# Attention with two feed-forward layers on one core: feed-forward products in whole blocks of four chunks, and attention's memory used again

## The chip, the core and the metric

One Trainium2 chip, one of its eight cores. The metric is the device time of one execution in microseconds; the median of several runs is compared. A profile is one execution more, taken by the hardware profiler. Engines: TensorE (PE, its weight loads PEld), VectorE (DVE), ScalarE (ACT), GpSimd (POOL), and the sync queue (SP), which issues the DMAs.

## What is computed

Block-sparse attention (2 x 8 heads, 768 positions, head size 64; a local window of 16 plus 24 block summaries of keys and values), then two feed-forward layers of 1,536 tokens, 512 wide, 2,048 hidden:

```python
x = attention(q, k, v)              # (B*S, H*D) = (1536, 512)
h = x @ w_in;  g = h * clip(h + 3, 0, 6) / 6;  x = g @ w_out     # first layer
h = x @ w_in2; g = h * cos(h);                 out = g @ w_out2  # second layer
```

Inputs are float64 for the weights. Each operand of a feed-forward product is split in a rounded high part and a low part, and three matmuls (high x high, high x low, low x high) stand for one product.

## The kernel before

**Tiling.** Tokens are cut in 3 blocks j of 512, the 2,048 hidden columns in 16 chunks of 128, and the chunks in 4 groups g of 4. The feed-forward work is a list of items (layer L, group g, block j, chunk c), lines 696 to 706: for each layer, for each group, for each block, the 4 chunks. The first block's items are cut in half, and so is the very last item (`cut`). With 2 layers x 4 groups x 3 blocks there are 24 blocks of 4 chunks.

**One item.** `g1` (line 728) is the first product: 4 steps of 3 matmuls (lines 738 to 740) into one PSUM bank `h` or `a`. `post` (line 747) turns the bank into the two parts of g: in the second layer ScalarE scales (L770), a rounding step on GpSimd or VectorE (L782), two VectorE steps (L774), two on ScalarE (L770), a VectorE product with the bank (L788), a rounded copy on ScalarE or GpSimd (L357, L359: high part) and a subtraction on VectorE or GpSimd (L364: low part). `g2` (line 796) is the second product: for each of 4 banks `acc`, 3 matmuls (line 815). A bank adds up over the 4 chunks of a block; after the fourth chunk `evac` (line 824) copies it (L357) or adds it (L837) to a part in SBUF, and at a layer's last group splits it for the next layer or sends it out.

**Weights.** `weights` (line 656) loads each chunk's two halves (`w_in`, `w_out`) as float64 words and builds high and low float32 parts: ScalarE (L676) and VectorE (L680, L685) into `cf`, a copy (L357 or L359) and a subtraction (L364) into `w`. Half 0 serves the first product, half 1 the second. All three blocks of a group use the same 4 weight tiles.

**Buffers.** PSUM has 8 banks: 4 `acc`, 2 `h`, 2 `a`. In SBUF there are 6 weight tiles `w` (`GS + 2`), 3 tiles `g`, one `n` and one `r` (odd items use `kr` and `va` of attention in their place), 2 `raw`, one `cu`, one `cf`. All are in one pool `cp` for the whole kernel.

**What sets the order.** Nothing is scheduled on the chip. Every operation is given to a planner (`Plan`) with the engines it may run on, a duration for each, a priority (smaller is earlier), what it reads and writes, and the buffers that it takes. `order` (line 221) runs a list scheduler over these durations; `refine` repeats it with due times as priorities for all but TensorE's operations and keeps the best plan; `run` (line 303) writes the instructions in that order, and each engine carries out its own in that order, waiting where it must. Priorities of the feed-forward work come from `vt` (line 710): item n of the list has a time, `IT` = 5.2 apart; its first product has that time, its second product that plus `pp` and `lag1` or `lag2` (line 859). So first and second products of single chunks take turns, with the second some items behind:

```python
for n, it in enumerate(items):
    pr = vt(it)
    h = g1(it, pr, late)
    gb = post(it, h, pr + T["pp"], late)
    g2(it, gb, pr + T["pp"] + T["lag2" if L else "lag1"])
```

Attention is 24 units of two query tiles, with priorities `A0 + AS * ...` (lines 624 to 650); feed-forward items of the first blocks fill in between. Token block 2 needs the last units.

Of the kernel before, what the change touches and what calls it, by code (L numbers as in the profile page):

```python
# [18 lines left out]
P = 128  # L19
# [28 lines left out]
def consts():  # L48
# [17 lines left out]
    late=16, cut=1, d0=0.9, warm=9, tail=1, qa=1, na=10, vy=3, split=1, lagq=0, nz=3, nq=3, nraw=2, ncf=1, n=5,  # L66
# [21 lines left out]
class Slots:  # L88
    def __init__(self, tiles, fifo=True, bank=False):
        self.tiles, self.fifo, self.bank = tiles, fifo, bank  # L90
        self.free = list(range(len(tiles)))
        self.made = self.given = 0


class Op:
    __slots__ = ("engs", "fn", "prio", "seq", "wait", "after", "ready", "takes", "uses", "start", "eng", "took")


class Plan:


    AFTER = {"PE": 0.2, "ACT": 0.145, "DVE": 0.13, "POOL": 0.1, "DMA": 0.95}
    TO_PE = {"PE": 0.0, "ACT": 0.28, "DVE": 0.25, "POOL": 0.15, "DMA": 0.95}
    LOAD = {"PE": 1.0, "ACT": 1.0, "DVE": T["DVE"], "POOL": T["POOL"], "DMA": 1.0}

    def __init__(self):
        self.ops, self.writer, self.readers = [], {}, {}

    def op(self, engs, fn, prio, r=(), w=(), take=()):
        o = Op()  # L110
        o.engs, o.fn, o.prio, o.seq = engs, fn, prio, len(self.ops)
# [36 lines left out]
    def reset(self):  # L148
        for o in self.ops:
            o.wait, o.ready, o.start, o.eng = 0, 0.0, None, None  # L150
            for x in o.uses:
                x.uses = 0
                x.slot = None
                x.cls.free = list(range(len(x.cls.tiles)))
                x.cls.given = 0
# [65 lines left out]
    def order(self):  # L221
# [13 lines left out]
        push(T["d0"], "free", None)  # L235
        for o in self.ops:
            if not o.wait:
                push(0.0, "ready", o)
        order = []
        while events:  # L240
            now = events[0][0]
            while events and events[0][0] <= now + 1e-9:
# [4 lines left out]
                elif what == "release":  # L247
                    x.cls.free.append(x.slot)
            for e in names:
# [28 lines left out]
                cost = o.engs[e] * (2.0 if e == "PE" and now < T["cold"] else 1.0)  # L278
                o.start, o.eng = now, e
# [9 lines left out]
                push(free[e], "free", None)  # L289
                for a in o.after:  # L290
# [12 lines left out]
    def run(self):  # L303
        self.refine()
        for o in self.order():
            o.fn(o.eng)


@with_exitstack
def body(ctx: ExitStack, tc: tile.TileContext, q, k, v, w_in1, w_out1, w_in2, w_out2, ident_d, mask_d, avg_d, out):  # L310
# [4 lines left out]
    pp = ctx.enter_context(tc.tile_pool(name="pp", bufs=1, space=bass.MemoryType.PSUM))  # L315

    def slots(name, n, shape, dtype=F32, fifo=True, pool=cp):
        return Slots([pool.tile(shape, dtype, name=f"{name}{i}") for i in range(n)], fifo, pool is not cp)

    ident = cp.tile([P, P], F32, name="ident")  # L320
    mask = cp.tile([P, 3, NK + CK], F32, name="mask")
    avg = cp.tile([P, AW], F32, name="avg")
# [7 lines left out]
    c_qz = slots("qz", T["nz"], [P, 2, HT * P])  # L330
    c_vc = slots("vc", 4, [P, TB, P])
    c_kr = slots("kr", 2, [P, TB, P])
    c_qr = slots("qr", T["nq"], [P, HT, P])
# [3 lines left out]
    c_vt = slots("vt", 1, [96, 4, D])  # L337
    c_e = slots("e", 4, [P, 2, NE])
    c_sm = slots("sm", 6, [P, 4])
    c_pt = slots("pt", 3, [P, 3, P])  # L340
# [41 lines left out]
    op = pl.op  # L382

# [5 lines left out]
    def load_consts():  # L389
# [9 lines left out]
        op({"POOL": 1.13}, variants, T["mask"], r=["mask"], w=["masks"])  # L399
# [31 lines left out]
    def fill_vc(b, p, vc, prio):  # L431
        for o in range(2):
            f = slice(D * o, D * o + D)
            rr = slice(32 + 32 * o, 64 + 32 * o)
            op({"POOL": 0.48},
# [6 lines left out]
    def vsum_pe(b, p, va, prio):  # L442
# [8 lines left out]
        op({"PE": 0.215 * TB}, mm, prio, r=["avg", (va, 0), (va, 1)], w=[bank], take=[bank])  # L451
        for o in range(2):
            f = slice(D * o, D * o + D)
            op({"ACT": 0.11, "DVE": 0.13}, lambda e, f=f: copy(e, vs[b][f, p, :], bank.t[f, f]), prio,
               r=[bank], w=[("vs", b, p, o)])

    def vsum(b, hh, prio):
        src = v[b, 4 * hh:4 * hh + 4].rearrange("h (n t) d -> (h n) (t d)", t=BLK)
        vt = Buf(c_vt)
        for u, (t0, n) in enumerate(((0, 12), (12, 12), (24, 8))):  # L460
# [7 lines left out]
            op({"DVE": 0.07 + 0.067 * n},  # L468
# [19 lines left out]
    def k_prep(b, p, kr, prio, banks):  # L488
# [33 lines left out]
        op({"POOL": 1.5}, edges, prio + 0.2, r=[(kw, "own", t0) for t0, _ in KCUT], w=[(kw, "edge")])  # L522
# [5 lines left out]
        op({"POOL": 0.56}, sums, prio + 0.2, r=[(ks, t0) for t0, _ in KCUT], w=[(kw, "sum")])  # L528
# [16 lines left out]
    def att(b, t, p, kw, z, va, vc, prio, banks):  # L545
# [18 lines left out]
        for o in range(2):  # L564
# [17 lines left out]
            {"POOL": 0.16},  # L582
# [8 lines left out]
            {"POOL": 0.755, "DVE": 0.455},  # L591
# [4 lines left out]
            prio, r=[(sm, 2), (sm, 3)], w=[(e_, 0), (e_, 1)],  # L596
# [8 lines left out]
        op({"ACT": 0.37, "DVE": 0.46},  # L605
# [13 lines left out]
        op({"ACT": 0.16, "DVE": 0.2}, lambda e: copy(e, hi, tp.t[:, 3 * P:4 * P]), prio, r=[(tp, 1)],  # L619
           w=[("xh", j, p, i)])  # L620
        op({"DVE": 0.2}, lambda e: sub(e, lo, tp.t[:, 3 * P:4 * P], hi), prio, r=[(tp, 1), ("xh", j, p, i)],
# [29 lines left out]


# [3 lines left out]
    def weights(c, prio):  # L656
# [3 lines left out]
        for half in range(2):  # L660
# [7 lines left out]
            else:  # L668
# [6 lines left out]
            op({"ACT": 0.52},  # L675
# [7 lines left out]
               prio, r=[raw], w=[f], take=[f])  # L683
            op({"DVE": 0.6},
# [4 lines left out]
            op({"POOL": 0.6, "ACT": 0.52}, lambda e, f=f, a=a: copy(e, w.t[:, 0, a], f.t), prio, r=[f],  # L689
               w=[(w, half, 0)], take=[w])  # L690
            op({"POOL": 1.23, "DVE": 0.6}, lambda e, f=f, a=a: sub(e, w.t[:, 1, a], f.t, w.t[:, 0, a]), prio,
               r=[f, (w, half, 0)], w=[(w, half, 1)])
# [35 lines left out]
    def g1(it, pr, late):  # L728
# [4 lines left out]
        for kk in range(KT):  # L733
# [8 lines left out]
            op({"PE": 0.65 * (y - x) / TOK}, mm, pr,  # L742
# [4 lines left out]
    def post(it, hb, pr, late):  # L747
# [21 lines left out]
        def act(func, out, in_, pr, fixed, rd, wr, take=(), **kw):  # L769
            op({"ACT": t(fixed, 0.425)}, lambda e: nc.scalar.activation(out=out(), in_=in_(), func=func, **kw), pr,  # L770
               r=rd, w=wr, take=take)

        def stt(s, out, a, b, o0, o1, rd, take=()):
            op({"DVE": t(0.07, 0.53)}, lambda e: nc.vector.scalar_tensor_tensor(  # L774
# [5 lines left out]
        else:  # L780
            act(ACTF.Identity, n, h, pr, 0.146, [hb], [nb], [nb], scale=1.0 / (2.0 * math.pi), bias=bias[:, 1:2])
            op({"POOL": t(0.16, 0.43), "DVE": t(0.07, 0.265)}, lambda e: eng[e].tensor_scalar(  # L782
                out=n(), in0=n(), scalar1=1.0, scalar2=-MAGIC, op0=ALU.mult, op1=ALU.add), pr, w=[nb])
            stt(-C1, r, n, h, ALU.mult, ALU.add, [nb, hb], [rb])
            stt(-C2, r, n, r, ALU.mult, ALU.add, [nb])
            act(ACTF.Abs, r, r, pr, 0.094, [], [rb])
            act(ACTF.Sin, r, r, pr, 0.185, [], [rb], scale=-1.0, bias=bias[:, 2:3])
            op({"DVE": t(0.07, 0.53)}, lambda e: nc.vector.tensor_tensor(out=r(), in0=r(), in1=h(), op=ALU.mult),  # L788
               pr, r=[hb], w=[rb])
        op({"ACT": t(0.095, 0.425), "POOL": t(0.16, 0.43)}, lambda e: copy(e, hi(), r()), pr, r=[rb], w=[(gb, 0)],  # L790
           take=[gb])
        op({"DVE": t(0.07, 0.53), "POOL": t(0.15, 1.08)}, lambda e: sub(e, lo(), r(), hi()), pr,
           r=[rb, (gb, 0)], w=[(gb, 1)])
        return gb

    def g2(it, gb, pr):
        L, g, j, c, x, y = it
        w = wb[L * NCH + g * GS + c]
        for m in range(4) if L == 0 else range(x // P, y // P):
# [18 lines left out]
            op({"PE": 0.65 * (1 if L else (y - x) / TOK)}, mm, pr,  # L818
# [5 lines left out]
    def evac(L, g, j, m, acc, pr):  # L824
        key, pt, take = part_of(j, m)
        if g == 0:
            op({"ACT": 0.48, "DVE": 0.6}, lambda e: copy(e, pt(), acc.t), pr, r=[acc], w=[key], take=take)
# [13 lines left out]
        if L == 0:  # L841
            hi, lo = xh[j][:, m, :], xl[j][:, m, :]
            op({"ACT": 0.52, "POOL": 0.6}, lambda e: copy(e, hi, pt()), pr, r=[key],
               w=[("xh", j, m, i) for i in range(QT)])
            op({"DVE": 0.6, "POOL": 1.23}, lambda e: sub(e, lo, pt(), hi), pr,
               r=[key, *(("xh", j, m, i) for i in range(QT))], w=[("xl", j, m, i) for i in range(QT)])
# [3 lines left out]

    for n, it in enumerate(items):
        L, g, j, c, x, _ = it
        pr = vt(it)
        if j == 0 and x == 0:
# [4 lines left out]
        g2(it, gb, pr + T["pp"] + T["lag2" if L else "lag1"])  # L859

    pl.run()

# [21 lines left out]
```

## Time and profile before

| | |
|---|---|
| time, median of 3 runs | 667.12 us (666.59 to 668.02) |
| profiled execution: its own time | 668.72 us |
| profiled execution: span, first to last instruction | 666.9 us |
| mean granted TensorE clock | 0.992 |
| TensorE matmuls busy | 641.6 us, 96% of the span |
| VectorE busy | 406.1 us, 61% |
| ScalarE busy | 346.1 us, 52% |
| GpSimd busy | 308.8 us, 46% |

Matmul records are longer than the time from one to the next, since matmuls are pipelined; starts are to be compared, not lengths. A busy share is a mean over stages that have different limits, so it is read by stage. "<-" behind a row names what an engine waited for last.

### The profile page before, as it was taken

To read this page: it belongs to the slowest core of one execution; us is meant where nothing else is said; L and a number is where in the kernel's file an instruction comes from. 1 tells how busy PE (TensorE), PEld (TensorE's weight loads), DVE (VectorE), ACT (ScalarE), POOL (GpSimd) and SP (SyncE) were. 2 spreads that over 40 slices of the span, in tenths; PEclk is the share of its full clock that TensorE was granted. 3 is DMA by queue.
4 is the path that set the end of the run, shared out by engine and by line. 5 is a ranking of instruction groups with operands and counts; after the bars stand their busy time and mean duration, and the time that the engine had idled before them with its cause. 6 is when DMAs were issued, how large, how long until landed. Compare 5 with 4: busy or idle time off the path is not lost.

```text
span 666.9 us, 9353 instructions
## 1 busy us (share of the span) xinstructions
PE 641.6 (96%) x3198; PEld 528.5 (79%) x3198; DVE 406.1 (61%) x808; ACT 346.1 (52%) x752; POOL 308.8 (46%) x411
## 2 busy tenths in 40 slices
PE   8999899999999999999999989997989999999997
PEld 7878788887888888888888868886868877787885
DVE  4789866542355146514661887558765886576655
ACT  5988688774353234323442555556644545444342
POOL 6678685443254235423552663235632564344232
PEclk8999999999999999999999989999989999999999
DMA  8775764000053003301420143004300331000103
GB/s 175 193 209 151 179 168 116 9 1 1 2 157 95 0 32 127 95 0 35 135 84 1 31 127 94 1 0 127 102 25 0 96 100 59 1 31 1 63 9 119
DMA packets 66031, 49.28 MB, mean 74 GB/s; under 512 B 42880, under 2 KB 59904, under 8 KB 65984
## 3 DMA queue, kind: packets, MB, share of 16 engines
q1 hardware_dynamic: 65840, 48.63, 25.6%
q8 instruction: 25, 0.41, 0.3%
q14 instruction: 22, 0.18, 0.1%
q10 hardware_dynamic: 144, 0.07, 0.0%
HBM read 45.48 MB, written 3.15 MB: 73 GB/s over the span
## 4 chain that ended last, share of the span: by engine, by line
PE 48%; DVE 26%; ACT 12%; issue 6%; POOL 6%; DMA 1%; SPq 1%; DVEq 0%; ACTq 0%; POOLq 0%
PE acc L815 19%; DVE va L774 4%; DVE r L774 4%; PE h L738 4%; PE h L740 4%; PE h L739 4%; ACT va L770 3%; ACT r L770 3%; POOL w L364 3%; DVE cf L685 3%; DVE cf L680 3%; PE a L740 2%; PE a L739 2%; PE a L738 2%; PE a L556 2%
## 5 line engine op out<-in xcount | busy, mean ns | idle before, releaser
L815 PE MATMUL acc<-w,g 128*128 128x512 f32 x576 | 144.5, 399 | 12.9 <-DVE part L837 4.8
L815 PE MATMUL acc<-g,w 128*128 128x512 f32 (+1 forms) x624 | 145.7, 377 | 0.5 <-POOL g L364 0.5
L815 PEld LDWEIGHTS acc<-w,g 128*128 128x128 f32 x576 | 108.8, 191 | 41.7 <-DVE part L837 6.7
L815 PEld LDWEIGHTS acc<-g,w 128*128 128x128 f32 x624 | 111.5, 188 | 22.0 <-issue 1.4
L364 POOL TENSOR_TENSOR g<-r,g 128x512 fp32r<-128x512 f32 (+1 forms) x51 | 68.0, 1333 | 64.7 <-ACT g L357 63.9
L738 PE MATMUL h<-xh,w 128*128 128x512 f32 (+1 forms) x236 | 92.0, 390 | 0.0
L739 PE MATMUL h<-xl,w 128*128 128x512 f32 (+1 forms) x236 | 88.1, 373 | 0.0
L740 PE MATMUL h<-xh,w 128*128 128x512 f32 (+1 forms) x236 | 88.1, 373 | 0.0
L364 POOL TENSOR_TENSOR w<-cf,w 128x512 fp32r<-128x512 f32 x45 | 61.9, 1375 | 48.1 <-ACT w L357 46.2
L364 POOL TENSOR_TENSOR g<-va,g 128x512 fp32r<-128x512 f32 (+1 forms) x32 | 42.9, 1340 | 63.2 <-ACT g L357 62.4
L774 DVE SCALAR_TENSOR_TENSOR r<-n,h 128x512 f32<-128x512 f32 (+1 forms) x59 | 37.8, 640 | 49.6 <-ACT n L770 42.0
L740 PE MATMUL a<-xh,w 128*128 128x512 f32 (+1 forms) x168 | 65.1, 387 | 0.6 <-POOL w L364 0.6
L738 PE MATMUL a<-xh,w 128*128 128x512 f32 (+1 forms) x168 | 65.1, 387 | 0.1
L739 PE MATMUL a<-xl,w 128*128 128x512 f32 (+1 forms) x168 | 65.0, 387 | 0.0
L680 DVE TENSOR_SCALAR cf<-raw 128x512 uint32<-128x512 uint32 x64 | 41.3, 645 | 31.8 <-POOL w L364 31.0
L357 ACT ACTIVATE w<-cf 128x512 fp32r<-128x512 f32 x44 | 27.8, 631 | 57.7 <-DVE cf L685 57.6
L676 ACT ACTIVATE cu<-raw 128x512 f32<-128x512 f32 x64 | 42.5, 664 | 20.3 <-DVE cf L685 20.2
L770 ACT ACTIVATE n<-h,bias 128x512 f32<-128x512 f32 (+1 forms) x59 | 38.1, 646 | 27.8 <-PE h L740 27.2
L738 PEld LDWEIGHTS h<-xh,w 128*128 128x128 f32 x236 | 44.7, 189 | 8.5 <-issue 0.7
L740 PEld LDWEIGHTS h<-xh,w 128*128 128x128 f32 x236 | 44.3, 188 | 7.8
L685 DVE SCALAR_TENSOR_TENSOR cf<-cu,cf 128x512 uint32<-128x512 uint32 x64 | 47.4, 740 | 4.9 <-ACT cu L676 1.2
L739 PEld LDWEIGHTS h<-xl,w 128*128 128x128 f32 x236 | 44.5, 188 | 7.3
(102 smaller groups left out, 1043.6 us busy)
## 6 DMA issues: line engine op xcount, KB each, us to landing
raw<-in_moe_w_in_dram SPq DMA_DIRECT2D x32, 512.0 KB, 3.8
raw<-in_moe_w_out_dram SPq DMA_DIRECT2D x32, 512.0 KB, 3.4
kr<-in_k_dram SPq DMA_DIRECT2D x16, 192.0 KB, 3.3
qr<-in_q_dram SPq DMA_DIRECT2D x48, 64.0 KB, 2.1
va<-in_v_dram SPq DMA_DIRECT2D x16, 192.0 KB, 4.6
out_dram<-part SPq DMA_DIRECT2D x8, 256.0 KB, 2.0
kr<-in_v_dram SPq DMA_DIRECT2D x4, 288.0 KB, 4.1
out_dram<-kw SPq DMA_DIRECT2D x3, 256.0 KB, 2.0
```

The costliest lines, as they stand in the source:

```text
L357: nc.scalar.activation(out=out, in_=in_, func=ACTF.Copy, scale=scale)
L364: eng[e].tensor_tensor(out=out, in0=in0, in1=in1.bitcast(F32), op=ALU.subtract)
L556: nc.tensor.matmul(out=sp.t[:, o * NK:o * NK + NK], lhsT=z.t[:, o, zi], rhs=kw.t[:, t, off(o):off(o) + NK], start=True, stop=True,)
L676: lambda e, raw=raw, u=u: nc.scalar.activation(out=u.t, in_=raw.t.bitcast(F32)[:, :, 1], func=ACTF.Prelu, scale=2.0 ** -112, alpha=2.0 ** 32),
L680: lambda e, raw=raw, f=f: eng[e].tensor_scalar(out=f.t.bitcast(U32), in0=raw.t[:, :, 0], scalar1=2.0 ** -29, scalar2=7.0, op0=ALU.mult, op ...
L685: lambda e, u=u, f=f: nc.vector.scalar_tensor_tensor(out=f.t.bitcast(U32), in0=u.t.bitcast(U32), scalar=3, in1=f.t.bitcast(U32), op0=ALU.l ...
L738: nc.tensor.matmul(out=o, lhsT=wh, rhs=hi, start=(kk == 0), stop=False)
L739: nc.tensor.matmul(out=o, lhsT=wh, rhs=lo, start=False, stop=False)
L740: nc.tensor.matmul(out=o, lhsT=wl, rhs=hi, start=False, stop=(kk == KT - 1))
L770: op({"ACT": t(fixed, 0.425)}, lambda e: nc.scalar.activation(out=out(), in_=in_(), func=func, **kw), pr, r=rd, w=wr, take=take)
L774: op({"DVE": t(0.07, 0.53)}, lambda e: nc.vector.scalar_tensor_tensor(out=out(), in0=a(), scalar=s, in1=b(), op0=o0, op1=o1), pr, r=rd, w= ...
L815: nc.tensor.matmul(out=o, lhsT=l, rhs=r, start=(c == 0 and z == 0), stop=(c == GS - 1 and z == 2))
```

## The change

From the fourth block on (`mo=3`) the four first products of a block get priorities half an item apart, and the second products of all four chunks get priorities behind the next block's first products, and bank by bank: all four chunks of bank 0, then of bank 1, and so on. The tiles that only attention uses (`mask`, `avg`, `qz`, `vc`, `qr`, `vt`, `e`, `pt`) move to a pool of their own, which is closed once the last attention operation has been written; in its place come 2 more weight tiles, 4 more `g`, one more `n` and one more `r`, which the planner may give out from that time on. The last item is no longer cut. And many durations in the planner are set anew (TensorE's second attention product from 0.45 to 0.684, for example), together with a surcharge `port` for some VectorE operations while GpSimd runs.

```diff
-    late=16, cut=1, d0=0.9, ..., n=5,
+    late=16, d0=0.9, ..., n=5, w2=2, nr2=1, g2=4, mo=3,
...
 class Slots:
+    def __init__(self, make, n, later, fifo=True, bank=False):
+        self.tiles = [make(i) for i in range(n)] + [None] * later
+    def more(self):
+        return range(self.n, len(self.tiles))
...
-    AFTER = {"PE": 0.2, "ACT": 0.145, "DVE": 0.13, "POOL": 0.1, "DMA": 0.95}
-    TO_PE = {"PE": 0.0, "ACT": 0.28, "DVE": 0.25, "POOL": 0.15, "DMA": 0.95}
+    AFTER = {"PE": 0.2, "ACT": 0.135, "DVE": 0.13, "POOL": 0.09, "DMA": 0.95}
+    TO_PE = {"PE": 0.0, "ACT": 0.2, "DVE": 0.19, "POOL": 0.15, "DMA": 0.95}
...
+                elif what == "turn":
+                    for cls in self.second:
+                        cls.free += cls.more()
...
+                if e == "DVE" and free["POOL"] > now + 0.1:
+                    cost += o.port
...
+                if o.seq < self.first:
+                    first -= 1
+                    opens = max(opens, end + self.AFTER[e])
+                    if not first:
+                        push(opens, "turn", None)
...
-    c_w = slots("w", GS + 2, [P, 2, 2 * DM], F32R)
-    c_n = slots("n", 1, [P, TOK])
-    c_r = slots("r", 1, [P, TOK])
-    c_g = slots("g", 3, [P, 2, TOK], F32R)
+    c_w = slots("w", GS + 2, [P, 2, 2 * DM], F32R, later=T["w2"])
+    c_n = slots("n", 1, [P, TOK], later=T["nr2"])
+    c_r = slots("r", 1, [P, TOK], later=T["nr2"])
+    c_g = slots("g", 3, [P, 2, TOK], F32R, later=T["g2"])
...
+    pl.second = [c_w, c_g, c_n, c_r]
+    def turn():
+        first.close()
+        pool = rest.enter_context(tc.tile_pool(name="lp", bufs=1))
+        for cls in pl.second:
+            for i in cls.more():
+                cls.tiles[i] = cls.make(i, pool)
...
-        op({"PE": 0.45}, pv, prio, r=[pt, *v_keys(va, vc)], w=[(tp, 1)])
+        op({"PE": 0.684}, pv, prio, r=[pt, *v_keys(va, vc)], w=[(tp, 1)])
...
-                for c in range(GS):
-                    last = (L, g, j) == (1, NG - 1, NBLK - 1) and c >= GS - T["cut"]
-                    cuts = (0, TOK // 2, TOK) if last else (0, TOK)
-                    items += [(L, g, j, c, x, y) for x, y in zip(cuts, cuts[1:])]
+                items += [(L, g, j, c, 0, TOK) for c in range(GS)]
...
+    block = []
     for n, it in enumerate(items):
         L, g, j, c, x, _ = it
+        whole = (L * NG + g) * NBLK + j >= T["mo"]
         pr = vt(it)
+        if whole:
+            pr = vt((L, g, j, 0, 0, TOK)) + c * IT / 2
         if j == 0 and x == 0:
             weights(L * NCH + g * GS + c, pr + T["wc"])
         h = g1(it, pr, late)
         gb = post(it, h, pr + T["pp"], late)
-        g2(it, gb, pr + T["pp"] + T["lag2" if L else "lag1"])
+        if not whole:
+            g2(it, gb, pr + T["pp"] + T["lag2" if L else "lag1"])
+            continue
+        block.append((it, gb))
+        if c == GS - 1:
+            pr = vt((L, g, j, 0, 0, TOK)) + 6 * IT
+            for m in range(KT):
+                for i, (it, gb) in enumerate(block):
+                    g2(it, gb, pr + (m + i / GS) * IT / 2, [m])
+            block = []
```

## Rows read from the trace of the kernel before

**Rows 1.** Windows by stage: length, busy us (records) by engine, granted clock, DMA.

```profile
0.00:90.00 90.00, 82.32 (x599) 71.11 (x601) 68.65 (x235) 69.35 (x221) 63.65 (x153) 0.98 0.74 180
90.00:162.10 72.10, 71.93 (x477) 59.55 (x478) 34.98 (x157) 50.68 (x163) 35.40 (x70) 1.00 0.20 53
162.10:382.42 220.32, 220.32 (x973) 182.51 (x972) 104.71 (x144) 86.27 (x139) 90.54 (x77) 1.00 0.19 60
400.00:645.00 245.00, 234.70 (x1015) 190.51 (x1014) 169.39 (x235) 122.42 (x199) 101.27 (x96) 0.99 0.15 48
```

**Rows 2.** Timeline of TensorE from 374: start, length, engine, line, operation, count.

```profile
374.26 0.39 PE L738 MATMUL a<-xh,w 128*128 128x512 f32 x1
...
376.98 2.88 PE L815 MATMUL acc<-g,w 128*128 128x512 f32 x12
379.70 0.39 PE L738 MATMUL h<-xh,w 128*128 128x512 f32 x1
```

**Rows 3.** Groups of TensorE from 382.42 on: count, busy us, mean ns, idle before.

```profile
L815 PE MATMUL acc<-w,g 128*128 128x512 f32 x576 | 144.5, 399 | 12.9 <-DVE part L837 4.8 <-ACT kw L357 3.4 <-DVE kw L837 3.2
...
L738 PE MATMUL a<-xh,w 128*128 128x512 f32 (+1 forms) x92 | 35.5, 386 | 0.1
...
L815 PE MATMUL acc<-g,w 128*128 128x512 f32 x24 | 5.8, 389 | 0.0
```

**Rows 4.** Timeline of TensorE, its last matmuls.

```profile
658.80 4.24 PE L815 MATMUL acc<-w,g 128*128 128x512 f32 x18
```

**Rows 5.** Waits of TensorE from 382.42 on: us in total, times, longest.

```profile
PE acc L815 <- DVE part L837: 4.8, 7, 1.4
PE acc L815 <- ACT kw L357: 3.4, 1, 3.4
PE acc L815 <- DVE kw L837: 3.2, 2, 1.9
PE acc L815 <- ACT g L357: 1.4, 1, 1.4
PE a L740 <- POOL w L364: 0.6, 1, 0.6
```

**Rows 6.** Timeline from 486 to 491, VectorE and TensorE's second products.

```profile
486.49 0.69 DVE L788 TENSOR_TENSOR va<-va,a 128x512 f32<-128x512 f32 x1 [1.45 <-ACT va L770]
487.09 0.68 DVE L837 TENSOR_TENSOR part<-part,acc 128x512 f32<-128x512 f32 x1
...
487.92 0.93 PE L815 MATMUL acc<-w,g 128*128 128x512 f32 x3 [1.02 <-DVE part L837]
...
488.53 1.03 DVE L782 TENSOR_SCALAR n<-n 128x512 f32<-128x512 f32 x1 [0.76 <-ACT n L770]
489.48 1.87 DVE L837 TENSOR_TENSOR part<-part,acc 128x512 f32<-128x512 f32 x3
490.21 3.91 PE L815 MATMUL acc<-w,g 128*128 128x512 f32 x9 [1.36 <-DVE part L837]
```

**Rows 7.** Window of the nine matmuls after that wait.

```profile
490.21:493.96 3.75, 3.75 (x9) 2.95 (x10) 2.43 (x4) 1.25 (x3) 0.00 (x0) 0.54 0.00 0
```

**Rows 8.** Timeline from 648, high and low part of one g.

```profile
648.57 0.63 ACT L357 ACTIVATE g<-va 128x512 fp32r<-128x512 f32 x1 [0.84 <-DVE va L788]
...
649.28 1.30 POOL L364 TENSOR_TENSOR g<-va,g 128x512 fp32r<-128x512 f32 x1 [4.70 <-ACT g L357]
```

**Rows 9.** Timeline of VectorE, first step of two weight halves in a row.

```profile
386.71 0.83 DVE L680 TENSOR_SCALAR cf<-raw 128x512 uint32<-128x512 uint32 x1 [1.45 <-POOL w L364]
391.51 0.41 DVE L680 TENSOR_SCALAR cf<-raw 128x512 uint32<-128x512 uint32 x1
```

**Rows 10.** Groups of VectorE from 400 to 645; timeline of VectorE at 389.

```profile
L774 DVE SCALAR_TENSOR_TENSOR r<-n,r 128x512 f32<-128x512 f32 x21 | 19.9, 948 | 0.6
...
L774 DVE SCALAR_TENSOR_TENSOR r<-n,h 128x512 f32<-128x512 f32 x21 | 14.3, 679 | 1.4 <-POOL n L782 1.1
389.80 1.79 DVE L364 TENSOR_TENSOR g<-va,g 128x512 fp32r<-128x512 f32 x1
```

More of the change, by code (lines that the diff above doesn't have):

```diff
@@ L65 @@
     wl=-8.0, wc=-11.4, g0=14.8, gi=21.5, lag1=18.2, lag2=14.2, pp=4.5, fill=31.9, vpe=-2.65, DVE=2.246, POOL=0.928, cold=5,
-    late=16, cut=1, d0=0.9, warm=9, tail=1, qa=1, na=10, vy=3, split=1, lagq=0, nz=3, nq=3, nraw=2, ncf=1, n=5,
+    late=16, d0=0.9, warm=9, tail=1, qa=1, na=10, vy=3, split=1, lagq=0, nz=3, nq=3, nraw=2, ncf=1, n=5, w2=2, nr2=1, g2=4, mo=3,
 )
@@ L88, with reset @@
 class Slots:
[L89 to L92, printed above, removed]
+    def __init__(self, make, n, later, fifo=True, bank=False):
+        self.make, self.n, self.fifo, self.bank = make, n, fifo, bank
+        self.tiles = [make(i) for i in range(n)] + [None] * later
+        self.made = 0
+        self.reset()
+    def reset(self):
+        self.free, self.given = list(range(self.n)), 0
+    def more(self):
+        return range(self.n, len(self.tiles))
 class Op:
-    __slots__ = ("engs", "fn", "prio", "seq", "wait", "after", "ready", "takes", "uses", "start", "eng", "took")
+    __slots__ = ("engs", "fn", "prio", "port", "seq", "wait", "after", "ready", "takes", "uses", "start", "eng", "took")
 class Plan:
-    AFTER = {"PE": 0.2, "ACT": 0.145, "DVE": 0.13, "POOL": 0.1, "DMA": 0.95}
-    TO_PE = {"PE": 0.0, "ACT": 0.28, "DVE": 0.25, "POOL": 0.15, "DMA": 0.95}
+    AFTER = {"PE": 0.2, "ACT": 0.135, "DVE": 0.13, "POOL": 0.09, "DMA": 0.95}
+    TO_PE = {"PE": 0.0, "ACT": 0.2, "DVE": 0.19, "POOL": 0.15, "DMA": 0.95}
     LOAD = {"PE": 1.0, "ACT": 1.0, "DVE": T["DVE"], "POOL": T["POOL"], "DMA": 1.0}
@@ L107, in __init__, with op @@
         self.ops, self.writer, self.readers = [], {}, {}
-    def op(self, engs, fn, prio, r=(), w=(), take=()):
+        self.first, self.second, self.turn = 0, [], None
+    def op(self, engs, fn, prio, r=(), w=(), take=(), port=0.0):
         o = Op()
-        o.engs, o.fn, o.prio, o.seq = engs, fn, prio, len(self.ops)
+        o.engs, o.fn, o.prio, o.port, o.seq = engs, fn, prio, port, len(self.ops)
         o.wait, o.after, o.ready, o.takes = 0, [], 0.0, list(take)
@@ L153, in reset @@
                 x.slot = None
-                x.cls.free = list(range(len(x.cls.tiles)))
-                x.cls.given = 0
+                x.cls.reset()
         for o in self.ops:
@@ L235, in order @@
         push(T["d0"], "free", None)
+        first, opens = self.first, 0.0
         for o in self.ops:
@@ L304, in run @@
         self.refine()
+        left = self.first
         for o in self.order():
             o.fn(o.eng)
+            if o.seq < self.first:
+                left -= 1
+                if not left:
+                    self.turn()
 @with_exitstack
@@ L315, in body, with slots @@
     pp = ctx.enter_context(tc.tile_pool(name="pp", bufs=1, space=bass.MemoryType.PSUM))
-    def slots(name, n, shape, dtype=F32, fifo=True, pool=cp):
-        return Slots([pool.tile(shape, dtype, name=f"{name}{i}") for i in range(n)], fifo, pool is not cp)
+    first = ExitStack()
+    ap = first.enter_context(tc.tile_pool(name="ap", bufs=1))
+    def slots(name, n, shape, dtype=F32, fifo=True, pool=cp, later=0):
+        return Slots(lambda i, pool=pool: pool.tile(shape, dtype, name=f"{name}{i}"), n, later, fifo, pool is pp)
     ident = cp.tile([P, P], F32, name="ident")
-    mask = cp.tile([P, 3, NK + CK], F32, name="mask")
-    avg = cp.tile([P, AW], F32, name="avg")
+    mask = ap.tile([P, 3, NK + CK], F32, name="mask")
+    avg = ap.tile([P, AW], F32, name="avg")
     bias = cp.tile([P, 4], F32, name="bias")
@@ L382, in body @@
     op = pl.op
+    pl.second = [c_w, c_g, c_n, c_r]
+    rest = ExitStack()
+    def turn():
[4 more added lines that the diff above has]
+                cls.tiles[i] = cls.make(i, pool)
+    pl.turn = turn
     def dma(out, in_, us, prio, r=(), w=(), take=()):
@@ L520, in edges @@
                 copy(e, kw.t[:, 0:TB - 1, u + WIN:u + 2 * WIN], own[:, 1:TB, 0:WIN])
-        op({"POOL": 1.5}, edges, prio + 0.2, r=[(kw, "own", t0) for t0, _ in KCUT], w=[(kw, "edge")])
+        op({"POOL": 1.7}, edges, prio + 0.2, r=[(kw, "own", t0) for t0, _ in KCUT], w=[(kw, "edge")])
         def sums(e):
@@ L581, in att @@
         op(
-            {"POOL": 0.16},
+            {"POOL": 0.2},
             lambda e: nc.gpsimd.tensor_scalar(
@@ L650, in body @@
             att(b, HT * h + i, p, kws[p], z, va, vc, pr + AS * i, c_acc if y < T["na"] else c_a)
+    pl.first = len(pl.ops)
     wb = {}
@@ L826, in evac @@
         if g == 0:
-            op({"ACT": 0.48, "DVE": 0.6}, lambda e: copy(e, pt(), acc.t), pr, r=[acc], w=[key], take=take)
+            op({"ACT": 0.485, "DVE": 0.6}, lambda e: copy(e, pt(), acc.t), pr, r=[acc], w=[key], take=take)
             return
@@ L858, in body @@
         gb = post(it, h, pr + T["pp"], late)
-        g2(it, gb, pr + T["pp"] + T["lag2" if L else "lag1"])
+        if not whole:
[8 more added lines that the diff above has]
+            block = []
     pl.run()
+    rest.close()
 _INS = ["q", "k", "v", "moe_w_in", "moe_w_out", "moe2_w_in", "moe2_w_out"]
```

79 lines of the change are left out of this document (40 added, 39 removed).

## The prediction

> **What bounds the kernel now.** I read the busy times by stage first, then TensorE's own order in time, then who it waited for. The stages [rows 1] show three different kernels. From 0 to 90 us (attention) TensorE is short of work: 82.3 us busy, so 7.7 idle, with VectorE and ScalarE at three quarters. From 90 to 382.4 it is busy throughout (0.2 us idle to 162.1, none at all in the 220.3 us after that, in which 973 records, one of them cut by the window's edge, are 81 groups of 12, all feed-forward work): this is its own pace, and nothing that other engines do counts. From 382.4, in the second feed-forward layer, it has holes again: 234.7 busy of 245 between 400 and 645.
>
> The pace can be read exactly. A first product of a chunk (12 matmuls of 512 columns) takes 374.26 to 376.98, a second product 376.98 to 379.70: 2.72 us each, 226.7 ns a matmul [rows 2]. The second product changes PSUM bank after every third matmul, the first stays in one bank, and both take the same; so going bank by bank gains nothing in itself.
>
> How far the rest is from that pace: from 382.42 on there are 576 + 24 second-product matmuls and six groups of first-product ones with 92 each (one counts 93, with a record that runs across the window's start), of which four in each are of half width, the two halves of the last chunk [rows 3]: 576 + 24 + 6 x 90 = 1,140 full ones, or 95 groups of 12. At 2.72 that is 258.4 us. The last matmul ends at 663.04 [rows 4]; less the 0.16 by which a record (0.39) outlasts its slot (0.227), TensorE took 662.88 - 382.42 = 280.5 us. **So 22.1 us lie above the pace**, all in the second layer. This is what the change can win there, and no more.
>
> What the 22.1 us are: the waits from 382 on name a PSUM bank `acc` almost only, not yet drained by VectorE (L837) or ScalarE (L357) [rows 5]. One place shows why [rows 6]. All four banks of a block close within one second product, 0.68 us apart, and bank 0 is wanted again after the other three (2.04) and one first product (2.72): 4.76 us. The drains stand in VectorE's queue behind another chunk's work: L788, which starts only at 486.49, then the first drain (487.09), then a 1.03 us step (488.53), then the other three (489.48). TensorE stands until 487.92 and again until 490.21. And then the clock is down: granted 0.54 of full speed, near the lower of its two levels (1.2 of 2.4 GHz), from 490.21 to 493.96, where nine matmuls take 3.75 us in place of 2.04 [rows 7]. The five waits of the list sum to 13.4 us [rows 5]; the other 8.7 are matmuls that start late or run slowly around them, as these nine do.
>
> **The change part by part.** *Order of the products.* From the fourth block on TensorE runs the four first products of block n+1 (10.88 us), then the second products of block n (10.88 us), bank by bank. Counted from the start of the second products, bank m closes at 2.72 x (m + 1) and is wanted again at 21.76 + 2.72 x m: 19.0 us in place of 4.76. The longest lateness in the list is 3.4 us [rows 5]; no drain can then be late. The same turn covers the g values: the last chunk's elementwise chain has the 10.88 us of another block's second products ahead of it. Value: all waits for `acc`, and the slow clock behind them: -22.1 if nothing new comes.
>
> *Four more g slots (3 to 7).* A block holds all four of its g until its last bank, so a whole block plus three chunks fit, and the fourth chunk of block n must wait. Counted from the start of block n's first products: block n-1's second products start at 10.88, and its first g is free after the first chunk of the last bank, 10.88 + 8.16 + 0.68 = 19.72. Then come the rounding copy (0.63) and the low part on GpSimd (1.30), with 0.08 us from one to the other [rows 8]: 21.8, say 22.0 at TensorE. It is wanted at 21.76 + 2.04 = 23.8. Margin 1.8 us; behind the waiting copy stands the rest of ScalarE's queue, and TensorE waits for the chain. No row of before shows this wait. Bounds: 0, or, where GpSimd has two 1.30 us steps ahead of it and ScalarE one of 0.63, (3.2 - 1.8) = 1.4 us for each of 20 blocks, 28 us. The margin covers one step ahead on each engine nearly whole (1.93), so I take a value near the low end: 1.0 us in all.
>
> *Two more weight slots (6 to 8), one more n and r.* Old weights are now held until the last bank of a group's last block, 19.72 us after the next group's start, so two groups must lie side by side: 8 slots are exactly that. After this the next weights have until their own start, 65.3 us after the group's (three blocks of 21.76); the seventh half (first half of chunk 3) is wanted 8.16 later, at 73.4. That leaves 53.7 us for 7 halves, 7.7 each. In the busiest stretch of before one half followed another after 4.8 us [rows 9], with the single cf buffer between them. Cost zero; the weight loads on the sync queue keep their number, and DMA is at 0.15 to 0.20 of its capacity here [rows 1].
>
> *Memory handed over.* The extra tiles lie where attention's were and wait for its last readers. Attention is over by 162.1, and TensorE has work at full pace there without them [rows 1]: zero.
>
> *The split of the last chunk is dropped.* Its post-processing lay open at the end; now block 23's lies behind block 22's second products. Included in the 22.1. After the last matmul the same adds and output remain: zero.
>
> *New durations in the planner.* They can reorder attention's 48 units. Bound: TensorE's idle time there, 7.7 us [rows 1], as a gain, and the same as a loss (an estimate, having no row). I take zero.
>
> *Engines' load.* Without its 15 us or so of holes the stretch 400 to 645 becomes 230 us, VectorE's 169.4 us in it 74%, ScalarE's 53%, GpSimd's 44% [rows 1]. None becomes the bound. Against this speaks that the two share something: VectorE's step with both inputs in SBUF takes 948 ns on average, the one with an input in PSUM 679, and single ones 1.79 us [rows 10]. If all 41 such steps of the stretch took 1.79, VectorE would carry about 35 us more, 204 of 230. Still no bound, but little room for queues. The Trainium skill, page "SBUF — State Buffer", section "Who interferes with whom", has this as a rule that speaks against more work in flight: a VectorE instruction with two SBUF inputs and a GpSimd one that reads SBUF shut each other out, and the second to come waits for the whole of the first. By that rule, the trace agrees (948 against 679); where it is paid in full it gives the first rival's time, where not, the sum above.
>
> **Sum.** Profiled execution: span 666.9 - 22.1 + 1.0 = 645.8. Its own time is 668.72, 1.6 above the median of the runs, 667.12. Taking the difference over: 667.12 - 21.1 = **646.0 us**.
>
> **The rivals.**
> (a) *The fourth g comes late.* ScalarE's and GpSimd's queues are in order, and 1.8 us are less than two steps. For it: the head-of-queue waits in [rows 6], the 1.79 us step in [rows 10]. Against: VectorE is the fuller engine, and the chain can use the other two. Half of the upper bound, 0.7 us x 20 = 14 us, in place of the 1.0: 659.
> (b) *Crowded queues, not banks.* Of the 13.4 us of waits, 5.4 name ScalarE or GpSimd (3.4 + 1.4 + 0.6). If those come from weight loads that crowd these queues, more room for drains doesn't cure them, and with their share of the slow matmuls 22.1 x 5.4 / 13.4 = 8.9 us stay: 655. For it: the longest of all, 3.4, is one of them. Against: four of the five name a bank or a g, and the new order gives 10 us and more to both.
> (c) *Slower: weights late.* If the extra slots don't give the lead, chunks 2 and 3 of a new group wait for old slots. TensorE then takes the old block's second products early, after two first products (5.44); a slot comes free 8.84 later, at 14.3; then two steps (0.63 + 1.30) and two more halves of 4.8 follow one after the other, to 25.8, while chunk 3 is wanted at 5.44 + 10.88 + 2.72 = 19.0. That is 6.8 us at each of 7 group starts, 48 us: 693. It decides once a half takes over 7.7 us in place of 4.8; each further us costs 7 at each start, 49 in all, so at 8.2 us the whole gain is gone. For it: the engines carry more side by side. Against: the 4.8 was measured in the most crowded stretch.
> (d) *Attention is reordered well too*, with most of its 7.7 us won: 639.
>
> **How the numbers follow.** Forecast (640.5 to 652) 0.71; (a) 0.09, (b) 0.06, (d) 0.05; attention worse by as much as is won, no change, 0.03; (c) 0.06. A measurement of this kernel tells about 0.2% from no change. Faster: 0.71 + 0.09 + 0.06 + 0.05 = 0.91, of which I give 0.01 to each of the other two for the long end of (a): 0.89, 0.04, 0.07. The range leaves out (d), the upper half of (a), (c) and no change: 640.5 to 660.
>
> **What would show it.** Right: from about 160 us to the end TensorE without holes, runs of 48 first- and 48 second-product matmuls at 10.88 us, no `acc` wait, granted clock 1.00, last matmul near 642. The fourth g's lateness would be waits of second products for `g`, once a block, in the first bank; late weights would be waits of first products for `w` every 65 us; crowded queues would be waits that name ScalarE or GpSimd while no bank and no slot is short. A changed pace would upset everything: the tiles of x, weights and g move in SBUF, and 1 ns on a matmul is 2.1 us over the 2,112 after 162 us; so far matmuls from different tiles all take 226.7. Attention's end, now at about 160 us, tells what the new durations did.

## The result and the profile after

| | before | after |
|---|---|---|
| time, median | 666.86 us (666.44 to 668.02, 4 runs) | 645.75 us (645.46 to 646.44, 4 runs) |
| ratio after / before | | 0.968, 95% interval 0.967 to 0.970 |
| span of the profiled execution | 666.9 us | 644.7 us |

The forecast was 646.0 us, with a range from 640.5 to 660. The windows by stage (columns as in [rows 1]) show the second layer as the first one was before: TensorE without a hole from the end of attention to its last matmul, granted clock 1.00 (the lines leave out 380 to 400).

```profile
0.00:90.00 90.00, 83.28 (x605) 72.04 (x605) 67.49 (x236) 72.03 (x231) 65.45 (x157) 0.98 0.77 186
90.00:162.10 72.10, 71.47 (x472) 58.97 (x471) 35.60 (x149) 51.23 (x167) 35.48 (x63) 1.00 0.17 48
...
162.06:380.00 217.94, 217.94 (x963) 180.44 (x962) 100.15 (x140) 92.67 (x152) 95.69 (x78) 1.00 0.21 68
400.00:641.00 241.00, 241.00 (x1064) 199.24 (x1062) 156.98 (x225) 130.25 (x209) 110.64 (x110) 1.00 0.17 56
```

The timeline of one turn of second products, TensorE and VectorE's drains (L874; L837 before):

```profile
466.76 11.04 PE L852 MATMUL acc<-w,g 128*128 128x512 f32 x48
...
471.97 0.68 DVE L874 TENSOR_TENSOR part<-part,acc 128x512 f32<-128x512 f32 x1
...
473.95 0.68 DVE L874 TENSOR_TENSOR part<-part,acc 128x512 f32<-128x512 f32 x1
...
476.45 0.68 DVE L874 TENSOR_TENSOR part<-part,acc 128x512 f32<-128x512 f32 x1
...
479.54 0.68 DVE L874 TENSOR_TENSOR part<-part,acc 128x512 f32<-128x512 f32 x1
```

48 matmuls follow one another for 10.88 us. Bank 0 closes at 466.76 + 2.72 = 469.48, its drain starts 2.5 us later, still behind other work as in [rows 6], and is over at 472.65; the bank is wanted again at 488.52, 16 us after that. The waits turn round: from 162 on the profile has no wait of TensorE at all, and VectorE's drains wait for TensorE (us in total, times, longest).

```profile
DVE part L874 <- PE acc L852: 32.4, 20, 2.0
...
DVE kw L874 <- PE acc L852: 23.4, 14, 2.0
```

**Above the pace.** To compare runs I use, as in the prediction, the time that TensorE took from 200 us to its last matmul, less 2.72 us for every 12 matmuls in it. What is left is the time in which TensorE waited or ran slowly, "above the pace", good to about 0.1 us. Before: 22.1 us. After: 0.0. The point from which 2,112 matmuls, all feed-forward work, are still to be done comes at 162.10 before and at 162.06 after; from the last matmul to the end of the span it was 3.87 and is 3.66 us. 22.1 + 0.0 + 0.2 = 22.3, the whole difference of the spans (22.2) within the rounding.

### The profile page after: what moved, and what is told of

It reads as the page before. It is cut to its first block, busy times and chain, and to the rows that moved or that the text cites. A ratio compares the mean times of both kernels' runs of the same rounds, so it can differ in the third digit from the quotient of the medians.

```text
span 644.7 us, 9290 instructions
## 1 busy us (share of the span) xinstructions
PE 633.7 (98%) x3186; PEld 527.2 (82%) x3186; DVE 377.8 (59%) x772; ACT 356.4 (55%) x773; POOL 319.0 (49%) x417
## 4 chain that ended last, share of the span: by engine, by line
PE 90%; DMA 3%; ACT 2%; POOL 2%; DVE 1%; issue 1%; SPq 1%; DVEq 0%; POOLq 0%; ACTq 0%
PE acc L852 40%; PE h L774 7%; PE h L776 7%; PE h L775 7%; PE a L775 6%; PE a L774 6%; PE a L776 6%; PE a L593 2%; PE a L651 2%; PE a L639 2%; PE a L648 1%; PE acc L593 1%; ACT e L612 1%; DMA qr<-in_q_dram 1%; DMA raw<-in_moe_w_in_dram 1%
## 5 line engine op out<-in xcount | busy, mean ns | idle before, releaser
L852 PE MATMUL acc<-g,w 128*128 128x512 f32 (+1 forms) x624 | 141.3, 378 | 0.0
L852 PE MATMUL acc<-w,g 128*128 128x512 f32 x576 | 132.3, 389 | 0.0
L390 POOL TENSOR_TENSOR g<-r,g 128x512 fp32r<-128x512 f32 (+1 forms) x47 | 59.9, 1274 | 59.3 <-ACT g L383 54.6
L390 POOL TENSOR_TENSOR g<-va,g 128x512 fp32r<-128x512 f32 x41 | 54.3, 1323 | 68.4 <-ACT g L383 59.2
L390 POOL TENSOR_TENSOR w<-cf,w 128x512 fp32r<-128x512 f32 x42 | 56.1, 1335 | 50.6 <-ACT w L383 50.3
L775 PE MATMUL a<-xl,w 128*128 128x512 f32 x168 | 65.4, 389 | 0.0
L774 PE MATMUL a<-xh,w 128*128 128x512 f32 x168 | 65.4, 389 | 0.0
L776 PE MATMUL a<-xh,w 128*128 128x512 f32 x168 | 65.4, 389 | 0.0
L383 ACT ACTIVATE g<-va 128x512 fp32r<-128x512 f32 x40 | 25.2, 631 | 58.7 <-PE acc L852 22.1
L724 DVE SCALAR_TENSOR_TENSOR cf<-cu,cf 128x512 uint32<-128x512 uint32 x64 | 51.8, 810 | 3.1 <-ACT cu L715 1.0
L874 DVE TENSOR_TENSOR part<-part,acc 128x512 f32<-128x512 f32 x48 | 32.7, 682 | 32.6 <-PE acc L852 32.4
```

The source lines that it names most:

```text
L383: nc.scalar.activation(out=out, in_=in_, func=ACTF.Copy, scale=scale)
L390: eng[e].tensor_tensor(out=out, in0=in0, in1=in1.bitcast(F32), op=ALU.subtract)
L724: lambda e, u=u, f=f: nc.vector.scalar_tensor_tensor(out=f.t.bitcast(U32), in0=u.t.bitcast(U32), scalar=3, in1=f.t.bitcast(U32), op0=ALU.l ...
L774: nc.tensor.matmul(out=o, lhsT=wh, rhs=hi, start=(kk == 0), stop=False)
L775: nc.tensor.matmul(out=o, lhsT=wh, rhs=lo, start=False, stop=False)
L776: nc.tensor.matmul(out=o, lhsT=wl, rhs=hi, start=False, stop=(kk == KT - 1))
```

## The experiments

The change has three parts: the order, the slots, and the planner's durations. The order and the slots were forecast to give everything, the durations nothing. The rival: the durations put the drains in the right place, and the order matters little. "Durations" are the planner's estimates, from which it fixes each engine's order; nothing on the chip takes another time for them. All runs are compared with the kernel before on the same chip; "above the pace" is from 200 us on.

| kernel | time | ratio to before | above the pace |
|---|---|---|---|
| before | 667 to 668 us | 1 | 22.1 |
| durations alone | 652.42 | 0.977 (0.976 to 0.979) | 5.1 |
| slots alone | 663.72 | 0.993 (0.991 to 0.996) | 18.0 |
| durations and slots, old order | 651.99 | 0.977 (0.975 to 0.978) | 4.8 |
| order, one more g slot, old durations | 656.13 | 0.983 (0.981 to 0.984) | 10.7 |
| order and slots, old durations | 645.37 | 0.967 (0.965 to 0.968) | 0.0 |
| all, second products chunk by chunk | 647.52 | 0.970 (0.968 to 0.972) | 0.0 |
| all, six weight slots | 648.28 | 0.970 (0.966 to 0.975) | 0.8 |
| all, four g slots | 646.54 | 0.968 (0.966 to 0.970) | 0.0 |
| before, TensorE's duration corrected | 677.85 | 1.014 (1.011 to 1.018) | 33.5 |
| durations alone, less TensorE's | 650.99 | 0.974 (0.971 to 0.977) | 3.6 |
| before, port surcharge alone | 654.27 | 0.980 (0.978 to 0.981) | 6.7 |
| before, durations between the two products alone | 661.54 | 0.989 (0.987 to 0.992) | 16.9 |

**The durations alone.** The last item is cut as before.

```diff
-    ..., w2=2, nr2=1, g2=4, mo=3,
+    ..., cut=1, w2=0, nr2=0, g2=0, mo=24,
```

> The new durations alone: order of single chunks as before, six weight and three g slots, the cut last chunk. Theory (the whole-block order takes TensorE's bank waits away): the second layer keeps its holes, with a bank acc as their name, 660 to 672 us; attention ends near 159 as in both kernels. Rival (the planner with measured durations puts the drains in the right place by itself, and the order does little): the holes shrink to a few us, 646 to 652 us.

Measured: 652.42 us, the rival's side, if just beyond its range. TensorE's waits from 380 on and the place that answers to [rows 6]:

```profile
PE acc L855 <- DVE part L877: 1.5, 1, 1.5
PE a L779 <- POOL w L390: 0.6, 1, 0.6
PE acc L855 <- DVE kw L877: 0.5, 1, 0.5
PE acc L855 <- ACT g L383: 0.3, 1, 0.3
```

```profile
478.26 0.69 DVE L828 TENSOR_TENSOR va<-va,a 128x512 f32<-128x512 f32 x1 [1.46 <-ACT va L809]
478.87 1.28 DVE L877 TENSOR_TENSOR part<-part,acc 128x512 f32<-128x512 f32 x2
479.69 3.37 PE L855 MATMUL acc<-w,g 128*128 128x512 f32 x12 [0.27 <-ACT g L383]
480.06 0.68 DVE L813 SCALAR_TENSOR_TENSOR r<-n,h 128x512 f32<-128x512 f32 x1
480.66 1.28 DVE L877 TENSOR_TENSOR part<-part,acc 128x512 f32<-128x512 f32 x2
```

The four drains (L877) still stand behind L828, but two follow it at once and the others come 0.5 us after them, in place of the 1.7 us between the first and the rest in [rows 6]. TensorE waits 0.27 us here, where it waited 1.02 and 1.36 and then ran at half clock. So the old order, with its 4.76 us between closing and next use, does not force the loss: 17 of the 22.1 us went with another plan of the same order.

**The slots alone, and slots with durations.** The first has the old durations, the second the new ones; in both the order of single chunks and the cut last item stay.

```diff
-    ..., w2=2, nr2=1, g2=4, mo=3,
+    ..., cut=1, w2=2, nr2=1, g2=4, mo=24,
```

> The kernel before with the extra slots alone (eight w, seven g, two n, two r from attention's end), old durations, order of single chunks. Theory (slots don't help drains that stand behind other work, and the plan is as wrong as before): 660 to 669 us, holes with a bank as the name. Rival (more slots loosen the queues): under 657 us.

> New durations and the extra slots (eight w, seven g, two n and r) with the order of single chunks as before. Theory (bank waits): the four banks still close within 2.7 us and are wanted again 4.8 us after closing, so holes stay: within 4 us of the run with the durations alone, 658 to 670 us. Rival (the slots are what was lacking: group starts and crowded queues): most of the 22 us go, 646 to 651 us.

Measured: 663.72 and 651.99 us; the slots take 4.1 us off the old plan's 22.1 and 0.3 off the new one's 5.1. The second run lies within 4 us of the durations alone, as expected, but not in the range of 658 to 670, which took it that those keep the holes. What TensorE waits for in the first has the names of [rows 5]:

```profile
PE acc L853 <- DVE part L875: 3.6, 7, 1.3
PE acc L853 <- DVE kw L875: 3.5, 3, 3.1
PE acc L853 <- ACT kw L381: 2.7, 1, 2.7
PE acc L853 <- ACT g L381: 0.8, 1, 0.8
```

The waits for drains sum to 9.8 us, where [rows 5] has 11.4. More slots alone hardly cure drains.

**Order and slots with the old durations.** All durations and hand-over times of the planner as before, the port surcharge off; two of some 30 lines:

```diff
-                if e == "DVE" and free["POOL"] > now + 0.1:
-                    cost += o.port
...
-            op({"PE": 0.03 + 0.65 * (y - x) / TOK}, mm, pr,
+            op({"PE": 0.65 * (y - x) / TOK}, mm, pr,
```

> Order and slots as after, all planner durations as before (port surcharge off). Theory (slack of 19 us on a bank and about 2 us on the fourth g makes the plan robust to wrong durations): 644 to 651 us, no bank waits; attention's end within 3 us of 159. Rival (the durations do a good part): over 655 us, with waits back in the second layer.

Measured: 645.37 us, and not one wait of TensorE after 162:

```profile
162.00:380.00 218.00, 218.00 (x964) 180.50 (x963) 109.31 (x146) 90.84 (x149) 93.73 (x76) 1.00 0.21 67
400.00:637.00 237.00, 237.00 (x1048) 196.23 (x1046) 163.08 (x228) 128.30 (x206) 105.36 (x105) 1.00 0.17 54
```

With the order and its slots the same wrong durations cost nothing that the pace shows. The two cures overlap: 17.0 us by the durations and 22.1 by order and slots, where only 22.1 are to be had.

**The order with hardly any memory.** Old durations, six w, one n, one r, and four g, since a block holds four at once.

```diff
-    ..., w2=2, nr2=1, g2=4, mo=3,
+    ..., w2=0, nr2=0, g2=1, mo=3,
```

> The order of whole blocks with the old durations and nearly no extra memory: four g slots (a block needs four at once), six w, one n and one r. Theory (the order alone makes the plan robust, the slots only widen it): 645 to 655 us, no waits for banks. Rival (order and slots only work together): over 658 us, with waits for g at the first bank of most blocks.

Measured: 656.13 us, between the two. The longest of the waits from 380 on:

```profile
PE a L772 <- DVE va L823: 2.0, 3, 0.7
PE a L774 <- POOL w L388: 1.1, 1, 1.1
PE h L772 <- DVE r L823: 0.9, 1, 0.9
```

The order does what was reckoned: no wait for a drain is left. But 10.7 us remain, and they have other names: first products wait for the banks `a` and `h`, which the elementwise chain (L823, the product with the bank) gives back late, and for weights. With the old durations, then, the second half takes the slots. Which of them, and whether the new durations would do in their place, is open: this run took all away at once, and no run has few slots and the new durations. Six weight slots or four g slots alone (below, with the new durations) cost under 1 us, so the single n and r are the candidate.

**Bank by bank or chunk by chunk.**

```diff
-            for m in range(KT):
-                for i, (it, gb) in enumerate(block):
-                    g2(it, gb, pr + (m + i / GS) * IT / 2, [m])
+            for i, (it, gb) in enumerate(block):
+                for m in range(KT):
+                    g2(it, gb, pr + (i + m / KT) * IT / 2, [m])
```

> As after, but a block's second products go chunk by chunk (four banks each) and not bank by bank; whole blocks still take turns. Theory (whole blocks give the slack, 10.88 us of first products between the close of the banks and their next use): no holes before the last block, 645 to 648 us, the end up to 2 us longer, since four banks close in the last 2.7 us. Rival (bank by bank is what spreads the drains and is needed): bank waits at most blocks, over 655 us.

Measured: 647.52 us, nothing above the pace. The four banks close within 2.7 us again, and 10.88 us of first products are enough for the drains. Of the 1.45 us between the spans 1.23 lie ahead of this: the first product that follows attention's last matmuls starts at 160.55 in place of 159.32, because the plan came out a little different; 0.22 are the end (3.88 against 3.66). So it is the whole blocks that count, not the banks.

**Six weight slots; four g slots.** Each is one number of the kernel after. They test two steps of the prediction, its slower rival and the fourth g.

```diff
-    ..., w2=2, nr2=1, g2=4, mo=3,
+    ..., w2=0, nr2=1, g2=4, mo=3,     (six weight slots)
+    ..., w2=2, nr2=1, g2=1, mo=3,     (four g slots)
```

> As after, but without the two extra weight slots (six in all). Prediction's slower rival, worked out for this case: chunk 3 of a new group late by 6.8 us at each of 7 group starts, 48 us, or 693 us, with waits of first products for w. If old weights are free sooner than I reckon, or the planner brings enough other work forward: 646 to 660 us.

> As after, but four g slots in place of seven (weights, n and r as after). By the prediction's reckoning each block's g can only start when the one before gives its own back, 1.9 to 2.1 us before they are wanted, with a chain of 2.2 us and 1.3 us on GpSimd for each further one: some 2 us late at each of 20 blocks, 680 to 690 us. If the planner brings first products forward to cover it: 646 to 652 us.

Measured: 648.28 and 646.54 us; neither price was there. With six weight slots TensorE's order itself is another one, since the planner knows the slots too. Two first products into a new group (it starts at 239.04) 51 second-product matmuls follow one another, three more than a block has, and 21 more come after a single first product:

```profile
244.48 11.72 PE L852 MATMUL acc<-g,w 128*128 128x512 f32 x51
...
258.76 4.92 PE L852 MATMUL acc<-g,w 128*128 128x512 f32 x21
263.52 0.39 PE L774 MATMUL a<-xh,w 128*128 128x512 f32 x1
```

By their number, 48 of the 51 are the old block's, and 3 + 21 = 24 belong to the two chunks of the new block whose first products are done. They give TensorE work while the old weights come free; the first product of the new group's last chunk follows at 263.52, without a wait. It costs 0.8 us above the pace, and 0.8 at attention's end (160.14 in place of 159.32). With four g slots the order is that of the kernel after, and the timeline shows the g of one block being made when the block before gives its own back:

```profile
257.63 0.63 ACT L383 ACTIVATE g<-r 128x512 fp32r<-128x512 f32 x1 [8.09 <-DVE kw L874]
...
258.34 1.51 POOL L390 TENSOR_TENSOR g<-r,g 128x512 fp32r<-128x512 f32 x1 [17.75 <-ACT g L383]
...
259.81 3.45 POOL L390 TENSOR_TENSOR g<-va,g 128x512 fp32r<-128x512 f32 x2
...
270.35 0.84 PE L852 MATMUL acc<-g,w 128*128 128x512 f32 x3
```

ScalarE stands 8.09 us before the first g, GpSimd 17.75, and still all four are there at 263.3 (one low part is made on VectorE), 7 us before TensorE takes the first at 270.35.

**Which durations.** Four kernels, all with the old order and slots: TensorE's feed-forward step corrected alone (0.65 to 0.68), all new durations but that one, the port surcharge alone, and the steps between first and second product alone. One line of each, but for the second, which takes the first back from the durations alone:

```diff
-            op({"PE": 0.65 * (y - x) / TOK}, mm, pr,
+            op({"PE": 0.03 + 0.65 * (y - x) / TOK}, mm, pr,
...
+                if e == "DVE" and free["POOL"] > now + 0.1:
+                    cost += o.port
...
-            op({"DVE": t(0.07, 0.53)}, lambda e: nc.vector.scalar_tensor_tensor(
+            op({"DVE": t(0.09, 0.56)}, lambda e: nc.vector.scalar_tensor_tensor(
```

> The kernel before with one thing changed: the planner's duration of a feed-forward step of three matmuls, 0.65 to 0.68 (measured 2.72 / 4). Theory A (the plan ran ahead because its TensorE was 4% too fast; drains were planned earlier than banks really close): most of what the durations gave alone comes from this, 652 to 657 us. Theory B (the plan ran ahead on the elementwise engines, so work in front of the drains came late): still 663 to 668 us.

> All new durations but the two of the feed-forward steps on TensorE (0.65 as before); order of single chunks, slots as before. Theory A (TensorE's duration): little of the gain is left, 661 to 668 us. Theory B (durations of VectorE, ScalarE, GpSimd and the port surcharge): most of it, 651 to 656 us.

> The kernel before with the port surcharge alone (VectorE steps planned 0.45 to 0.6 us longer while GpSimd runs), all other durations old, order of single chunks, slots as before. Theory C (the plan missed the time in which VectorE and GpSimd shut each other out): most of the gain of the durations, 650 to 656 us. Theory D (the small corrections of the elementwise steps count): 661 to 668 us.

> The kernel before with the new durations of the elementwise steps between first and second product alone (3 to 9% longer each), no surcharge. Theory C (port surcharge): still 660 to 669 us. Theory D (small corrections): 650 to 657 us. A third outcome, slower than before, would say that any change of the plan moves this order by some us either way.

Measured: 677.85, 650.99, 654.27 and 661.54 us. TensorE's right duration alone makes the kernel slower, by 1.4%, which neither theory had. The drains' waits grow (columns as in [rows 5]):

```profile
PE acc L815 <- DVE part L837: 10.2, 8, 2.6
PE acc L815 <- ACT part L357: 3.6, 3, 1.8
PE acc L815 <- DVE kw L837: 3.3, 3, 1.7
PE acc L815 <- ACT kw L357: 2.5, 1, 2.5
```

They are 8.0 us with the durations between the products alone,

```profile
PE acc L815 <- DVE kw L837: 3.6, 2, 2.3
PE acc L815 <- DVE part L837: 3.3, 3, 2.1
PE acc L815 <- ACT kw L357: 1.1, 1, 1.1
```

2.3 with the surcharge alone,

```profile
PE acc L855 <- DVE part L877: 1.6, 1, 1.6
...
PE acc L855 <- DVE kw L877: 0.5, 1, 0.5
PE acc L855 <- ACT part L383: 0.2, 1, 0.2
```

and none is left with all but TensorE's correction, where the longest wait is for a g:

```profile
PE acc L855 <- POOL g L390: 1.5, 1, 1.5
```

So the time above the pace goes with the waits for drains: 19.6, 11.4 (before), 8.0, 2.3 and 0 us of them with 33.5, 22.1, 16.9, 6.7 and 3.6 us.

The elementwise durations carry the gain: the surcharge alone takes 15.4 of the 22.1 us off, the small corrections alone 5.2, both and the rest without TensorE's 18.5. The surcharge stands for time that is really there. In the kernel before, from 162 us on, the 28 first steps of a weight half on VectorE (`cf<-raw`) that overlapped no GpSimd instruction took 422 ns on average, the 23 that did 948 ns.

A plan in which elementwise work is too short compared with TensorE's puts work in front of drains that in truth comes late; correcting TensorE alone widens that gap. That reading fits all four signs, but no run shows the planned times of drains beside the measured ones, so it is argued and not shown. Each of these kernels is one plan, too, and how much of a difference is the luck of that plan is not known. The eight plans in the old order lie anywhere between 3.6 and 33.5 us above the pace. The five with whole blocks and one more n and r lie between 0.0 and 0.8, whatever else was changed.

## Why the prediction was right, and where it was not

**The pace and the bound: right.** 22.1 us above 2.72 us per 12 matmuls was the size of what can be won, and 22.1 were. The start of pure feed-forward work (taken as unchanged) moved by 0.04 us. The memory handed over cost nothing that shows.

**The drains: right as to what goes, incomplete as to what it needs.** From "no drain can then be late" the prediction went on to all 22.1 us. The order with hardly any memory shows that this half holds to the letter (no drain is waited for) and is worth 11.4 us; the other 10.7 took the slots as well, with the old durations. The slow clock was a small part of the loss: the granted clock fell twice after 382, for 3.4 us each, and the matmuls in these two stretches came some 0.2 us late each, about 3 us together.

```profile
394.90:398.30 3.40, 3.40 (x10) 2.63 (x9) 3.40 (x5) 1.83 (x4) 3.40 (x4) 0.50 0.28 63
490.48:493.88 3.40, 3.40 (x9) 2.63 (x9) 2.16 (x4) 1.17 (x3) 0.00 (x0) 0.50 0.00 0
```

**The new durations: the step that failed.** "They can reorder attention's 48 units ... I take zero." They were looked at for attention only. They also order VectorE's queue in the second layer, where the prediction itself had found the drain behind L788 and a 1.03 us step. Alone they are worth 17.0 us there. The forecast hit all the same because the two cures share one loss, and the order with slots needs no durations (645.37).

**The fourth g: a slip in the count.** The prediction wanted it at 21.76 + 2.04 and put the margin at 1.8 us. But between a block's first products and its second lie a turn of second products, a turn of first ones: 10.88 x 3 + 2.04 = 34.7, so the margin was 12.7. Four slots without any wait confirm it. The 1.0 us taken for it, and rival (a), had no ground; without it the sum gives 645.0, so the last 0.7 us of the hit are luck.

**Weights.** Zero with eight slots: right. The price of rival (c), 48 us where the lead is missing, was wrong by far: 0.8 us. The count let TensorE bring the old block's second products forward, and nothing else, so chunk 3 came out 6.8 us late at each group. The planner also brings 24 second-product matmuls of the new block forward (5.44 us). Chunk 3's first product then starts 24.5 us after the group (263.52 - 239.04), near the 25.8 that rival (c) reckons for its weights, and nothing waits.

**Rival (b), crowded queues.** With order and slots nothing is left, so it is out for the kernel after. Where memory is short, weights do come late: the order with hardly any memory waits 1.1 us for a `w`. Whether crowded queues or missing slots make it late is not shown.

**Bank by bank** was said to gain nothing in itself: right, 0.0 above the pace with it and without it.

**Load and the shared inputs.** VectorE carries 157.0 of 241 us, 65%, less than the 74% reckoned; ScalarE (130.3 us) and GpSimd (110.6) carry more than in [rows 1]. Its two steps of [rows 10], now from 400 to 645:

```profile
L810 DVE SCALAR_TENSOR_TENSOR r<-n,r 128x512 f32<-128x512 f32 x21 | 15.5, 736 | 0.3
...
L810 DVE SCALAR_TENSOR_TENSOR r<-n,h 128x512 f32<-128x512 f32 x21 | 14.3, 681 | 19.9 <-POOL n L818 19.9
```

The form with two SBUF inputs costs 736 ns now, not 948, with the other one unchanged. What the prediction feared, that more work in flight brings more meetings with GpSimd, did come about; they only cost less each. From 400 us on there are 43 of these steps in either kernel, counting the form `va<-kr,va` too. Before, 22 of them overlapped a GpSimd instruction and took 1,067 ns on average; after, 33 did and took 821. The others took 687 and 685, like the form with a PSUM input. The trace agrees, so far, with the rule of the Trainium skill, page "SBUF — State Buffer", section "Who interferes with whom", by which a VectorE step with two SBUF inputs and a GpSimd one that reads SBUF shut each other out. Why a meeting costs less now is open; with order and slots and the old durations it is 905 ns.

## What to carry to other kernels

Where the order of each engine is fixed ahead, a late drain has two cures: place it by measured durations, or give the buffer so much time between closing and next use that its place doesn't matter. Here the first alone won 17.0 us of 22.1 and the second, with the slots that it needs, all of them; their gains don't add, so try each part of such a change by itself before saying which one did it. The second also made the result stand against other changes of the plan, where the old order swung by 30 us. Count the busiest engine's pace first: it bounds all of them together, and here it gave the size while the cause was only half seen.

## What the runs showed that was not expected

A more correct duration can make a planned kernel slower: with TensorE's step at its measured 0.68 and everything else as before, 677.85 us against 667.66.

The length of a single wait did not tell whether TensorE's clock fell. In the kernel before, its longest wait, 3.43 us, was followed by 12 matmuls in 2.87 us at a granted clock of 1.00, while waits of 1.02 and 1.36 us in a row were followed by 0.54 [rows 7]. The timeline and the window after the long wait:

```profile
464.82 1.43 PE L815 MATMUL acc<-w,g 128*128 128x512 f32 x5 [3.43 <-ACT kw L357]
```

```profile
464.82:467.69 2.87, 2.87 (x12) 2.34 (x13) 2.64 (x3) 2.19 (x5) 1.46 (x2) 1.00 0.44 154
```
